# Turning the first queries by full-height TensorE transposes, with fewer small products ahead of them

## The chip, the cores and the metric

The program runs on one core of one Trainium2 chip. The metric is the device time of one execution in microseconds (us), taken from several executions of the same program. A profiled execution gives the trace, in which every instruction of the core has a start and a duration. TensorE (PE) multiplies matrices and writes into PSUM, VectorE (DVE) and ScalarE (ACT) copy, add and evaluate functions, GpSimd (POOL) adds, and the DMA queues move data between main memory and SBUF. The trace also has one record for every DMA packet, those that bring a core its own instructions included.

## The reference

A linear attention block comes first, then two dense layers with a leaky ReLU between them. Batch and heads are 8 and 8, the sequence has 576 positions and the head 64 columns; the dense layers go from 512 to 2048 and back for 4608 tokens. Both weight matrices arrive as 64-bit floats, because a 32-bit array is multiplied by a 64-bit scalar.

```python
def _attn_ref(q, k, v, g_norm):
    kv = np.einsum('bhsd,bhse->bhde', k, v)
    out = np.einsum('bhsd,bhde->bhse', q, kv)
    rms = np.sqrt(np.mean(out * out, axis=-1, keepdims=True) + 1e-06)
    return (out / rms * g_norm).astype(np.float32)

def _moe_ref(x, w_in, w_out):
    h = x @ w_in
    g = np.maximum(0.01 * h, h)
    return (g @ w_out).astype(np.float32)

def reference(**kwargs):
    ...
    attn_out = _attn_ref(**attn_kwargs)
    # bridge: (B,H,S,D) -> (B*S, H*D)
    B, H, S, D = attn_out.shape
    x = np.ascontiguousarray(attn_out.transpose(0, 2, 1, 3)).reshape(B * S, H * D)
    return _moe_ref(x=x, **moe_kwargs)
```

## The kernel before

The first batch of attention stands alone at the start, because no dense layer can run before its result is there. TensorE contracts over partitions, so the product of q with kv needs q with its 64 head columns on the partitions. Later batches get that from a DVE transpose; the first one gets it from TensorE. The heads go in pairs `p` (four of them), two heads `l` in a pair, and a pair's tile `q_in` holds the two heads on partitions 0 to 63 and 64 to 127, with 9 (`J`) rows of 64 columns on each partition.

```python
def load_first():                      # cut: the tiles' homes
    for way, to, src, ts, p in (
            ("a", q_ins, q, qs, 0), ("s", q_ins, q, qs, 1), ("a", q_ins, q, qs, 2),
            ("s", q_ins, q, qs, 3), ("a", k_ins, k, ks, 0), ("s", v_ins, v, vs, 0),
            ("g", k_ins, k, ks, 1), ("g", v_ins, v, vs, 1), ("a", k_ins, k, ks, 3),
            ("s", v_ins, v, vs, 3), ("g", k_ins, k, ks, 2), ("g", v_ins, v, vs, 2)):
        ...
        to[0, p] = load_two({"a": nc.scalar, "s": nc.sync, "g": nc.gpsimd}[way],
                            src[0, 2 * p:2 * p + 2], ts[p])

zeros = view(g_all[0], 0, NT)          # NT = 512
nc.vector.memset(zeros[:, :64], 0.0)
nc.vector.memset(zeros[:, 64:], 0.0)
...
def half_of(p, i):                     # which half of the partitions a head's result takes
    return i ^ (p & 1)

def attention_kv(b, m, kv_ps):         # kv of the pairs 2m and 2m+1: 36 products of 64x64
    two = [(k_ins.pop((b, p)), v_ins.pop((b, p)), p) for p in (2 * m, 2 * m + 1)]
    for j in range(J):
        for i in range(2):
            for k_in, v_in, p in two:
                r, c = 64 * i, 64 * half_of(p, i)
                matmul(kv_ps[p % 2][c:c + 64, m, :], lhsT=k_in[r:r + 64, j, :],
                       rhs=v_in[r:r + 64, j, :], start=(j == 0), stop=(j == J - 1))
```

The first attention begins with products of zeros, which raise TensorE's clock, then turns q, forms kv, and goes on to the normalised result x. Every result of a product passes through PSUM and is copied from there.

```python
def first_attention():
    idle = ps_m.tile([P, NT], F32, tag="hd", name="idle_ps")

    def keep_warm(to=idle):
        matmul(to, lhsT=zeros[:, :P], rhs=zeros, start=True, stop=True)

    for _ in range(15):
        for i in range(4):
            r = slice(E * i, E * i + E)
            matmul(idle[r, :64], lhsT=zeros[r, :E], rhs=zeros[r, :64], start=True, stop=True)
    keep_warm()
    ...
    for p in range(NP):
        q_in = q_ins.pop((0, p))
        q_ps = ps_m.tile([P, J - 1, 64], F32, tag=("ha", "hb", "hc", "ha")[p], name="q_ps")
        for j in range(J):
            for l in range(2):
                r, c = slice(64 * l, 64 * l + 64), 64 * half_of(p, l)
                matmul((q_ps[:, j, :] if j < J - 1 else rest[p % 2][:, p // 2, :])[c:c + 64],
                       lhsT=q_in[r, j, :], rhs=ident[r, r], start=True, stop=True)
        to = qT[:, p, :].rearrange("p (t j) -> p j t", j=J)
        h = J // 2
        nc.scalar.copy(to[:, :h, :], q_ps[:, :h, :])
        nc.vector.tensor_copy(to[:, h:J - 1, :], q_ps[:, h:, :])
    for i in range(2):
        nc.vector.tensor_copy(
            qT.rearrange("p a (t j) -> p a t j", j=J)[:, i::2, :, J - 1], rest[i])
    for m in range(2):
        if m:
            keep_warm()
        attention_kv(0, m, kv_ps)
    for j in range(3, 7):
        load_w(j)
    w0 = rounding(0)                   # 64-bit weights to 32-bit, a few ACT and DVE steps
    next(w0, None)                     # two ACT steps
    copy_kv(0, kv_ps)
    next(w0, None)
    ...                                # o_products: 32 products, q with kv, into four banks
    for l in range(2):
        square(0, l)                   # ACT
        keep(0, l)                     # DVE, two copies
        add_up(0, l)                   # TensorE, sums over the columns of a head
    next(w0, None)                     # DVE
    square(1, 0); add_up(1, 0)
    root(0); turn(0)                   # ACT, TensorE
    next(w0, None)                     # DVE
    invert(0)                          # DVE
    ...
    spread(0); add_up(1, 1); root(1); turn(1); keep(1, 0); keep(1, 1)
    scale(0, 0); invert(1); scale(0, 1); spread(1)
    for l in range(2):
        scale(1, l)
    for j in range(1, 5):
        round_w(j)
```

After this the first block of the dense layers runs with plain products (`h_ps`, `o_acc`), and later blocks with a scheme of seven products in place of eight.

Of the kernel before, what the change touches and what calls it, by code (L numbers as in the profile page):

```python
# [9 lines left out]
F32 = mybir.dt.float32  # L10
# [13 lines left out]
def kernel(  # L24
# [36 lines left out]
    nc = tc.nc  # L61
    B, H, S, D = q.shape
    DM, DF = w_in.shape
    P = 128
    NE = DM // P
    E = 32
    NP = H // 2
    J = S // 64
    T = S // 32
    NT = 4 * P  # L70
    NB = B * S // NT
    N2 = NT // 2
# [1 line left out]
    NC = DF // 2 // (U * P)  # L74
    SLOPE = 0.01
    EPS = 1e-6
    assert H * D == DM and S == 64 * J and D == 64 and 2 * E == D and H == 8 and NP * E == P and B * S == NB * NT
    assert DM // 2 == N2 and NE == 4

    consts = ctx.enter_context(tc.tile_pool(name="consts", bufs=1))  # L80
# [7 lines left out]
    ps_m = ctx.enter_context(tc.tile_pool(name="ps_m", bufs=1, space=bass.MemoryType.PSUM))  # L88

    pin = tc.keep_in_program_order  # L90
# [14 lines left out]
    def view(t, lo, *shape):  # L105
        n = 1
        for d in shape:
            n *= d
        t = t[:, lo:lo + n]
        names = "abcd"[:len(shape)]  # L110
        return t.rearrange(f"p ({' '.join(names)}) -> p {' '.join(names)}",
                           **dict(zip(names, shape))) if len(shape) > 1 else t
# [4 lines left out]
    def matmul(*args, **kw):  # L117
        pin(nc.tensor.matmul(*args, **kw))  # L118
# [4 lines left out]
    def half_of(p, i):  # L123


        return i ^ (p & 1)
# [58 lines left out]
    zeros = view(g_all[0], 0, NT)  # L185
    nc.vector.memset(zeros[:, :64], 0.0)
    nc.vector.memset(zeros[:, 64:], 0.0)
    ident = consts.tile([P, P], F32, name="ident")
# [33 lines left out]
    def load_f64(src, eng):  # L222
        a, n = src.shape[-2:]
        n //= 2
        raw = next(raw_homes).bitcast(U32).rearrange("p (n two) -> p n two", two=2)
        load(raw.rearrange("p (a n) two -> p a (n two)", a=a), src, eng)
        return raw
# [41 lines left out]
    def load_w(j, *eng):  # L269
        eng = eng or (nc.sync,)  # L270
        dst, src = w_jobs[j]
        if w_in.dtype == I64:
            w_raws[j] = load_f64(src.bitcast(U32), eng)
        else:
            load(dst, src, eng)

    def rounding(j):
        if w_in.dtype == I64:
            yield from round_f64(w_jobs[j][0], w_raws.pop(j))
# [43 lines left out]
    def kv_tiles():  # L323
        return [ps_att.tile([P, NP // 2, D], F32, tag="att", name="kv_ps") for _ in range(2)]
# [116 lines left out]
    def first_attention():  # L441


        idle = ps_m.tile([P, NT], F32, tag="hd", name="idle_ps")

        def keep_warm(to=idle):
            matmul(to, lhsT=zeros[:, :P], rhs=zeros, start=True, stop=True)

        for _ in range(15):
            for i in range(4):
                r = slice(E * i, E * i + E)
                matmul(idle[r, :64], lhsT=zeros[r, :E], rhs=zeros[r, :64], start=True, stop=True)
        keep_warm()
        qT = qTs[0] = work.tile([P, NP, S], F32, tag="qT", name="qT")
        kv_ps = kv_tiles()
        rest = [ps_m.tile([P, NP // 2, 64], F32, tag=t, name="rest_ps") for t in ("oc", "oa")]
        for j in range(1, 3):
            load_w(j)  # L460
        for p in range(NP):
            q_in = q_ins.pop((0, p))
            q_ps = ps_m.tile([P, J - 1, 64], F32, tag=("ha", "hb", "hc", "ha")[p], name="q_ps")
            for j in range(J):
                for l in range(2):
                    r, c = slice(64 * l, 64 * l + 64), 64 * half_of(p, l)
                    matmul((q_ps[:, j, :] if j < J - 1 else rest[p % 2][:, p // 2, :])[c:c + 64],
                           lhsT=q_in[r, j, :], rhs=ident[r, r], start=True, stop=True)
            to = qT[:, p, :].rearrange("p (t j) -> p j t", j=J)
            h = J // 2  # L470
            nc.scalar.copy(to[:, :h, :], q_ps[:, :h, :])
            nc.vector.tensor_copy(to[:, h:J - 1, :], q_ps[:, h:, :])
        for i in range(2):
            nc.vector.tensor_copy(
                qT.rearrange("p a (t j) -> p a t j", j=J)[:, i::2, :, J - 1], rest[i])
        for m in range(2):
            if m:
                keep_warm()
# [3 lines that stand above are left out]
        w0 = rounding(0)  # L482
# [5 lines that stand above are left out]
        x = block(0)  # L488

        o_ps = [[ps_m.tile([P, 2, N2], F32, tag=t, name="o_ps") for t in tags]  # L490
                for tags in (("hb", "hd"), ("oa", "oc"))]
        squares = [[spare(NT, "sq").rearrange("p (e n) -> p e n", e=2) for _ in range(2)]
                   for _ in range(2)]
        roots = [work.tile([P, 2, 2, NP], F32, tag="rms", name="roots", bufs=2) for _ in range(2)]
        flat = [work.tile([64, N2], F32, tag="t2k", name="flat", bufs=3) for _ in range(2)]
        sum_ps = [ps_att.tile([P, NT], F32, tag="att", name="sum_ps") for _ in range(2)]
        inv_ps = [ps_m.tile([P, 2, N2], F32, tag=t, name="inv_ps") for t in ("ha", "hc")]
        for half in range(2):
            for e in range(2):
                o_products(0, half * N2, half * N2 + N2, e,  # L500
                           [o_ps[half][l][:, e, :] for l in range(2)])

        def square(half, l):
            pin(nc.scalar.activation(squares[half][l], o_ps[half][l], func=AF.Square))

        def keep(half, l):
            for e in range(2):
                to, o = x[:, 2 * l + e, half * N2:half * N2 + N2], o_ps[half][l][:, e, :]
                if half == 0:
                    pin(nc.vector.tensor_scalar(to, o, g_sb[:, e:e + 1], None, op0=ALU.mult))  # L510
                else:
                    pin(nc.scalar.activation(to, o, func=AF.Copy, scale=g_sb[:, e:e + 1]))

        def add_up(half, l):

            for e in range(2):
                matmul(sum_ps[half][E * l:E * l + E, :N2], lhsT=group,
                       rhs=squares[half][l][:, e, :], start=(e == 0), stop=(e == 1))

        def root(half):  # L520

            pin(nc.scalar.activation(flat[half], sum_ps[half][:64, :N2], func=AF.Sqrt,
                                     scale=1.0 / D, bias=eps_sb[:64]))

        def turn(half):
            for t in range(2):
                matmul(turned(half)[:, t, :, :], lhsT=flat[half][:, t * P:t * P + P],
                       rhs=ident[:64, :64].rearrange("p (l i) -> p l i", l=2)[:, :, :NP],
                       start=True, stop=True)

        def turned(half):
            return sum_ps[half][:, N2:N2 + 4 * NP].rearrange("p (t l a) -> p t l a", t=2, l=2)

        def invert(half):
            pin(nc.vector.reciprocal(roots[half], turned(half)))

        def spread(half):

            for l in range(2):
                for t in range(2):  # L540
                    for p in range(NP):
                        matmul(inv_ps[half][E * p:E * p + E, l, t * P:t * P + P],
                               lhsT=roots[half][:, t, l, p:p + 1].to_broadcast([P, E]),
                               rhs=ident, start=True, stop=True)

        def scale(half, l):
            to = x[:, 2 * l:2 * l + 2, half * N2:half * N2 + N2]
            pin(nc.vector.tensor_tensor(
                to, to, inv_ps[half][:, l, :].unsqueeze(1).to_broadcast([P, 2, N2]), op=ALU.mult))

        for l in range(2):
            square(0, l)
            keep(0, l)
            add_up(0, l)
        next(w0, None)
        square(1, 0)
        add_up(1, 0)
        root(0)
        turn(0)
        next(w0, None)  # L560
        invert(0)
        for _ in w0:
            pass
        square(1, 1)
        spread(0)
        add_up(1, 1)
        root(1)
        turn(1)
        keep(1, 0)
        keep(1, 1)  # L570
        scale(0, 0)
        invert(1)
        scale(0, 1)
        spread(1)
# [4 lines that stand above are left out]
# [360 lines left out]
    x_sides, _, sums, _ = sides_x(1)  # L939
# [123 lines left out]
```

## Time and profile before

The time before is 942.53 us, the median of three executions (942.1 to 942.6). The profiled execution took 942.25 us, of which the program's instructions span 940.5 us.

| Engine | Busy us | Share of the span | Instructions |
|---|---|---|---|
| PE, matmul | 920.1 | 98% | 7076 |
| PE, weight load | 779.1 | 83% | 7076 |
| DVE | 616.0 | 65% | 992 |
| ACT | 327.5 | 35% | 659 |
| POOL | 317.7 | 34% | 318 |

One product of 32-bit numbers in the code stands as two matmul records and two weight loads in the trace, so 7076 records are half as many products. A group of matmul records can overlap in the trace, because small products in different parts of the array run side by side. A line of the timeline begins with the start and the length in us, and ends, in brackets, with the idle time before it and what the profile takes to have ended it. "issue" there is idle time in which the engine waited for nothing that the profile shows.

### The profile page before, as it was taken

To read this page: it belongs to the slowest core of one execution; us is meant where nothing else is said; L and a number is where in the kernel's file an instruction comes from. 1 tells how busy PE (TensorE), PEld (TensorE's weight loads), DVE (VectorE), ACT (ScalarE), POOL (GpSimd) and SP (SyncE) were. 2 spreads that over 40 slices of the span, in tenths; PEclk is the share of its full clock that TensorE was granted. 3 is DMA by queue.
4 is the path that set the end of the run, shared out by engine and by line. 5 is a ranking of instruction groups with operands and counts; after the bars stand their busy time and mean duration, and the time that the engine had idled before them with its cause. 6 is when DMAs were issued, how large, how long until landed. Compare 5 with 4: busy or idle time off the path is not lost.

```text
span 940.5 us, 17989 instructions
## 1 busy us (share of the span) xinstructions
PE 920.1 (98%) x7076; PEld 779.1 (83%) x7076; DVE 616.0 (65%) x992; ACT 327.5 (35%) x659; POOL 317.7 (34%) x318
## 2 busy tenths in 40 slices
PE   7999999999999999999999999999999999999997
PEld 5544447788998899889998999989988999899996
DVE  3866994576457876587657865687558745654554
ACT  3544633242134332533343323342344232223320
POOL 2000364977522532236221611172225322532222
PEclk9999999999999999999999999999999999999999
DMA  8989916885598679856895589658755675567632
GB/s 271 246 211 220 267 61 188 275 296 163 181 312 260 182 211 304 257 164 200 286 287 173 171 280 297 193 169 262 236 154 176 196 219 188 174 199 220 187 108 67
DMA packets 90067, 200.05 MB, mean 213 GB/s; under 512 B 9856, under 2 KB 42112, under 8 KB 89984
## 3 DMA queue, kind: packets, MB, share of 16 engines
q1 hardware_dynamic: 79392, 186.85, 66.3%
q10 hardware_dynamic: 10144, 10.88, 3.4%
q8 instruction: 56, 0.92, 0.4%
q0 software_dynamic: 448, 1.18, 0.3%
q14 instruction: 27, 0.22, 0.1%
HBM read 172.39 MB, written 26.48 MB: 211 GB/s over the span
## 4 chain that ended last, share of the span: by engine, by line
PE 86%; DVE 8%; DMA 3%; issue 1%; POOL 1%; ACT 1%; SPq 0%; DVEq 0%; ACTq 0%; POOLq 0%
PE o_a L118 21%; PE o_c L118 17%; PE h_ha L118 10%; PE h_hc L118 8%; PE h_hb L118 7%; PE h_hd L118 6%; PE o_acc L118 4%; PE h_ps L118 4%; PE kv_ps L118 2%; PE h_c L118 2%; PE h_d L118 2%; PE o_ps L118 1%; PE h_a L118 1%; DMA pairs<-in_v_dram 1%; DVE o L582 1%
## 5 line engine op out<-in xcount | busy, mean ns | idle before, releaser
L582 POOL TENSOR_TENSOR gs<-g 128x512 f32<-128x512 f32 x64 | 81.3, 1289 | 446.7 <-ACT g L753 446.7
L582 DVE TENSOR_TENSOR o<-o_c,o 128x512 f32<-128x512 f32 x85 | 58.5, 688 | 108.2 <-PE o_c L118 108.1
L753 ACT ACTIVATE g<-g 128x512 f32<-128x512 f32 x124 | 78.2, 631 | 122.9 <-DVE g L582 122.9
L118 PE MATMUL o_a<-pairs,gs 128*128 128x256 f32 x496 | 117.3, 379 | 0.0
L582 DVE TENSOR_TENSOR o<-o_a,o 128x512 f32<-128x512 f32 x100 | 68.7, 687 | 71.2 <-PE o_a L118 71.1
L817 ACT COPY w_all<-h_ha 128x512 f32<-128x512 f32 x84 | 48.7, 580 | 189.8 <-PE h_ha L118 181.0
L118 PEld LDWEIGHTS o_a<-pairs,gs 128*128 128x128 f32 x496 | 90.0, 190 | 9.9
L118 PE MATMUL o_a<-w,g 128*128 128x256 f32 x248 | 59.9, 384 | 4.7 <-DVE o L582 4.1
L118 PEld LDWEIGHTS h_ha<-stage,w_all 128*128 128x128 f32 x448 | 58.8, 192 | 2.9
L118 PE MATMUL o_c<-w,g 128*128 128x256 f32 x248 | 59.7, 383 | 0.0
L118 PE MATMUL o_c<-pairs,gs 128*128 128x256 f32 x248 | 59.2, 381 | 0.0
L118 PE MATMUL o_a<-pairs,g 128*128 128x256 f32 x248 | 59.2, 381 | 0.0
L118 PE MATMUL h_ha<-stage,w_all 128*128 128x128 f32 x448 | 59.0, 275 | 0.0
L118 PE MATMUL o_acc<-w,g 128*128 128x512 f32 x128 | 58.3, 598 | 0.7 <-ACT g L898 0.7
L118 PE MATMUL o_c<-w,gs 128*128 128x256 f32 x248 | 58.7, 379 | 0.0
L118 PE MATMUL h_ps<-xT,w_all 128*128 128x512 f32 (+1 forms) x136 | 57.9, 570 | 0.2 <-DVE w_all L255 0.2
L582 DVE TENSOR_TENSOR g<-g,pairs 128x512 f32<-128x512 f32 x84 | 55.6, 689 | 1.9
L118 PEld LDWEIGHTS o_a<-w,g 128*128 128x128 f32 x248 | 44.9, 190 | 13.9 <-DVE o L582 7.8
L582 POOL TENSOR_TENSOR pairs<-w_all 128x512 f32<-128x512 f32 x8 | 11.1, 1383 | 125.7 <-ACT cut L244 106.9
L118 PEld LDWEIGHTS o_c<-w,g 128*128 128x128 f32 x248 | 44.9, 190 | 8.4 <-issue 3.1
L118 PEld LDWEIGHTS o_a<-pairs,g 128*128 128x128 f32 x248 | 45.0, 190 | 6.5 <-DVE w_all L582 0.9
L118 PEld LDWEIGHTS o_c<-pairs,gs 128*128 128x128 f32 x248 | 44.9, 190 | 6.5 <-issue 1.4
(202 smaller groups left out, 1980.6 us busy)
## 6 DMA issues: line engine op xcount, KB each, us to landing
w_all<-w SPq DMA_DIRECT2D x196, 448.0 KB, 4.1
pairs<-w SPq DMA_DIRECT2D x56, 512.0 KB, 4.4
out_dram<-o ACTq DMA_DIRECT2D x36, 256.0 KB, 4.6
v_in<-in_v_dram SPq DMA_DIRECT2D x29, 288.0 KB, 5.3
k_in<-in_k_dram SPq DMA_DIRECT2D x28, 288.0 KB, 5.8
q_in<-in_q_dram SPq DMA_DIRECT2D x56, 144.0 KB, 6.1
q_in<-in_q_dram SPq DMA_DIRECT2D x56, 140.0 KB, 6.0
w<-stage SPq DMA_DIRECT2D x12, 512.0 KB, 4.5
```

Of the source, the lines that this page charges most:

```text
L118: pin(nc.tensor.matmul(*args, **kw))
L582: ins = eng.tensor_tensor(out_, a, b_, op=ALU.subtract if minus else ALU.add)
L753: nc.scalar.activation(t, t if src is None else src, func=AF.Prelu, alpha=SLOPE)
L817: nc.scalar.copy(q[:, at], banks[tag])
```

## The change

The first queries are turned by transposes that take both heads of a pair at once: 128 partitions by 64 columns become 64 partitions by 128 columns, in one instruction of TensorE's transpose kind. All of it lands on PSUM partitions 0 to 63, and the copies to SBUF move each head to the half of the partitions that it belongs to. The 60 small zero products in front are left out; a second wide zero product takes their place, and zero products of half the width stand between the pairs. The purpose is to shorten TensorE's stream of instructions before kv.

```diff
-        def keep_warm(to=idle):
-            matmul(to, lhsT=zeros[:, :P], rhs=zeros, start=True, stop=True)
-        for _ in range(15):
-            for i in range(4):
-                r = slice(E * i, E * i + E)
-                matmul(idle[r, :64], lhsT=zeros[r, :E], rhs=zeros[r, :64], start=True, stop=True)
+        def keep_warm(n=NT):
+            matmul(idle[:, :n], lhsT=zeros[:, :P], rhs=zeros[:, :n], start=True, stop=True)
+        keep_warm()
         keep_warm()
         ...
-        rest = [ps_m.tile([P, NP // 2, 64], F32, tag=t, name="rest_ps") for t in ("oc", "oa")]
+        rest = ps_m.tile([64, NP, P], F32, tag="oc", name="rest_ps")
         ...
+        def move(p, l, to, of):
+            c = 64 * half_of(p, l)
+            eng = (nc.scalar.copy, nc.vector.tensor_copy)[l]
+            eng(qT[c:c + 64, p, :].rearrange("p (t j) -> p j t", j=J)[:, to, :],
+                of[:, :, 64 * l:64 * l + 64])
         for p in range(NP):
             q_in = q_ins.pop((0, p))
-            q_ps = ps_m.tile([P, J - 1, 64], F32, tag=("ha", "hb", "hc", "ha")[p], name="q_ps")
+            banks = [ps_m.tile([64, 4, P], F32, tag=t, name="q_ps")
+                     for t in (("ha", "hb"), ("hc", "oa"))[p % 2]]
             for j in range(J):
+                to = banks[j // 4][:, j % 4, :] if j < 8 else rest[:, p, :]
+                pin(nc.tensor.transpose(to, q_in[:, j, :], ident))
+            if p + 1 < NP:
+                keep_warm(N2)
+            for i in range(2):
                 for l in range(2):
-                    r, c = slice(64 * l, 64 * l + 64), 64 * half_of(p, l)
-                    matmul((q_ps[:, j, :] if j < J - 1 else rest[p % 2][:, p // 2, :])[c:c + 64],
-                           lhsT=q_in[r, j, :], rhs=ident[r, r], start=True, stop=True)
-            to = qT[:, p, :].rearrange("p (t j) -> p j t", j=J)
-            h = J // 2
-            nc.scalar.copy(to[:, :h, :], q_ps[:, :h, :])
-            nc.vector.tensor_copy(to[:, h:J - 1, :], q_ps[:, h:, :])
-        for i in range(2):
-            nc.vector.tensor_copy(
-                qT.rearrange("p a (t j) -> p a t j", j=J)[:, i::2, :, J - 1], rest[i])
+                    move(p, l, slice(4 * i, 4 * i + 4), banks[i])
+        for p in range(NP):
+            for l in range(2):
+                move(p, l, slice(8, 9), rest[:, p:p + 1, :])
```

The kv products, their waits, the order of everything after them and all loads are as before.

## The prediction

> **What bounds the kernel now.** I read the table of stretches first (length in us; then for each engine busy us and instructions; clock, DMA share, GB/s).
>
> ```profile
> 0.00:32.00 32.00, 24.40 (x580) 18.81 (x580) 13.38 (x32) 14.12 (x27) 5.16 (x14) 1.00 0.89 262
> 32.00:150.00 118.00, 117.21 (x504) 52.78 (x505) 94.76 (x167) 51.40 (x107) 21.42 (x16) 1.00 0.78 199
> 150.00:900.00 750.00, 744.34 (x5812) 677.47 (x5811) 490.75 (x768) 256.24 (x517) 282.52 (x282) 1.00 0.71 220
> ```
>
> From 32 us on TensorE is busy 99% of the time, and the change touches nothing there. The first 32 us hold 7.6 us of TensorE's idle time, and only they can change. So the whole effect is the shift of the first dense product (h_ps, 28.16 us). Next I read TensorE's timeline of that stretch, and one window of the DMA packets.
>
> ```profile
> 1.06 4.35 PE L118 MATMUL idle_ps<-g 32*32 32x64 f32 x122 [1.06 <-DVE g L186]
> ...
> 9.27 0.27 PE L118 MATMUL q_ps<-ident,early 64*64 64x64 f32 x2 [1.09 <-issue]
> ...
> 11.34 1.38 PE L118 MATMUL kv_ps<-v_in,k_in 64*64 64x64 f32 x72 [0.68 <-DMA k_in<-in_k_dram]
> 12.65 1.12 PE L118 MATMUL idle_ps<-g 128*128 128x512 f32 x2
> 14.28 0.52 PE L118 MATMUL kv_ps<-pairs 64*64 64x64 f32 x8 [0.50 <-DMA pairs<-in_v_dram]
> 15.79 1.16 PE L118 MATMUL kv_ps<-pairs 64*64 64x64 f32 x64 [0.99 <-issue]
> 17.43 2.05 PE L118 MATMUL o_ps<-qT,kv 64*32 64x256 f32 x64 [0.48 <-DVE kv L321]
> 20.76 1.91 PE L118 MATMUL sum_ps<-sq,group 128*32 128x256 f32 x12 [1.28 <-ACT sq L504]
> ...
> 28.16 3.72 PE L118 MATMUL h_ps<-xT,w_all 128*128 128x256 f32 x16
> ```
>
> Two stops are "issue": in the middle of a pair of q at 9.27, and eight records into the second kv at 15.79, where no data is missing. A third is hidden: sum_ps at 20.76 is put down to ACT, yet the first square began at 18.70 and ended near 19.3. The packets of the instruction queue explain all three.
>
> ```profile
> q8 instruction: 1, 0.02, 6.0%
> ```
>
> That is the window from 13 to 14 us. The queue has one packet of 16,384 bytes at 6.98, 13.46, 18.37 and 23.50 us, each about 1.0 us long, and TensorE goes on some 1.3 to 1.4 us after the first three ended (7.98 to 9.27, 14.42 to 15.79, 19.39 to 20.76). Counted in the timeline, 223 matmul records stand before the first stop, 348 before the second, 476 before the third: 125 and 128 apart, which with a weight load each is 256 instructions of 64 bytes, one packet. So TensorE starves for instructions three times. From going on to the next packet took 4.19, then 2.58, then 2.74 us: the packet of a block is asked for when the block before it is entered.
>
> **What the Trainium skill says.** "Runtime: NRT & Kernel Launch", section "Instruction fetch mechanics", has blocks of 16 KiB, 256 instructions, fetched by the engine's own DMA queue one ahead; the trace agrees. It calls the crossing "mostly hidden"; here three crossings show, with small products used up faster than blocks come. "TensorE: Matmul & The Clock Gate", section "Terms", has a transpose mode four times faster for 32-bit data; no run here shows it yet, but each transpose compiles to one matmul and one weight load where a product needs two of each. Its Part 4 says that transposes don't count as activity for the clock. Its Part 1 gives half clock until about 3.4 us of activity; the trace grants the full clock at 4.09 us, after zero products from 1.06.
>
> **The change part by part.** Counts: zero products fall from 122 records to 4 + 3 x 2 = 10, q from 144 to 36 (36 transposes at one record each). Together 266 become 46, so TensorE's stream is 440 instructions, nearly two blocks, shorter before kv. The compiled program agrees: 6856 records in place of 7076.
>
> Block ends stay put in the stream: before, they lie at records 95 (128 less than 223), 223, 348 and 476. Counting waits in as well, record 93 of the changed kernel is the first end, 47 records into the first kv; the next is record 219, 27 of 64 into o_ps; the third is record 347, in the first h_ps; the fourth lies among long products of 0.43 us.
>
> Front: the wide zero product waits for the whole memset (ends 1.48), so starts near 1.5. Eight records of this width take 3.43 us in the first block, 0.43 each at full clock, so 0.86 at half clock; three of those and a short fourth reach to about 4.7. q's first pair lands at 4.69. So the transposes begin about 4.8 where q began at 5.34; nothing hangs on that.
>
> Turning: 16 copies of 64 partitions by 256 plus 8 small ones, half on each engine. A 128x256 copy takes 0.62 us on either engine; I take the same for 64 partitions, and 0.3 for a small one. ACT is issuing weight loads until about 6.2; eight copies at a pitch of 0.53 (three ACT squares take 1.57) end near 10.5. In the kernel before, a DVE copy starts when the ACT copy of the same bank ends (7.16 to 7.19), so I let DVE trail by one, to 11.2. The eight small ones share one tile and alternate: 11.2 + 7 x 0.3 = 13.3. The last transposes need the second pair's banks, free near 9.2, so TensorE is through by about 10. kv starts at 11.34 because k lands at 11.30. qT is needed by o_ps after 16. All of this stays hidden.
>
> Step 1, kv. The first end is crossed about 11.6, when nothing has to be fetched in a hurry. The second kv starts at 14.28 and runs through like the first: last operand lands at 14.42, 1.3 us more, done 15.75 instead of 17.01. Minus 1.26.
>
> Step 2, o_ps. Copies of kv take 0.42 as before: o_ps starts at 16.17. Its record 27 needs the block asked for at 11.6: 2.6 to 4.2 to the packet, 1.0 for it, 1.4 to go on, so 16.6 to 18.2, near 16.9 in the middle. Needed near 16.7. The first square needs 32 records, so about 17.4 without a stop. ACT has two rounding steps behind a weight that lands at 16.31; they ran from 16.41 to 17.63 and stay there. The first square moves from 18.70 to 17.63: minus 1.07.
>
> Step 3, sums. No block end stands before sum_ps any more. The DVE row sets the pace: square ends 18.26, four keeps (1.66), two rounding steps (1.1), so inversion at 21.0, where it was 23.32. TensorE's half (sum 19.45, root 0.47, turn and hop 0.96) is ready at 20.9. The sum of steps 1 to 3 is minus 2.3, and everything behind it (spread, second half, scaling) keeps its lengths: h_ps at 25.85.
>
> Afterwards: could the weights hold h_ps back? Weight jobs 1 to 6 landed at 17.91, 20.77, 23.00, 24.95, 27.73 and 29.68 and were taken up by ACT at 27.40, 28.53, 29.68, 30.82, 36.25 and 37.40; slack of over 5 us, and loads gated by kv move forward too. ACT waits for no weight's DMA between 28 and 150. The 0.73 us wait of o_acc at 143.15 hangs on a DVE chain which TensorE's own o_ps at 108 started, so it shifts along. 942.5 - 2.3 = 940.2.
>
> **The rivals.**
> - The fetch comes late. At the slowest seen (4.19 + 0.96 + 1.37 = 6.5 after 11.6) o_ps stops until 18.1, the first square is at about 18.5, and only step 3 remains: minus 1.2 to 1.4, about 941.2. For it: DMA is busy until 14.4. Against it: the later packets came after 2.6 to 2.7.
> - The clock falls. The zero products start later, and transposes may not count, so 4.9 to 11.3 us has only three pieces of 0.43 us of plain products. At half clock kv's second half (1.3), o_ps (2.0) and sums take up to twice as long: plus 1 to plus 4, about 942 to 945. Against it: by the steps above one of the added zero products falls into about every 3.4 us, and the clock here stayed full over 17.5 to 24 us with only about half the time busy.
> - Copies bind. With a 64-partition copy over 1 us, the turning would reach past 16 us and hold o_ps. The time would be about 942. Against it: 3 us of slack.
> - Nothing shows: kv is set by landing (14.42), so someone reading only the chain of waits would expect zero. The chain speaks against this, since the stop is after the landing.
>
> **Range and chances.** The main case, 65%, gives 940.0 to 940.4; the late fetch, 20%, about 941.2; the clock or copies, 15%, 942 and up. Executions differ by 0.25. I centre on 940.4 with 939.5 to 942.0. Two per cent are 18.9 us, more than all that the first 20 us hold, so chances of either side are one in a hundred or less.
>
> **What would show it.** Right: instruction packets near 14.5 and 20 only, no "issue" stop before kv's end, kv done near 15.8, sum_ps following the first square, h_ps near 25.9, and a span 2.3 shorter with equal lengths after it. Wrong: a stop of over 1 us in o_ps (step 2), a granted clock of 0.5 after 5 us, two matmul records for a transpose, ACT or DVE still copying q at 16 us, or an h_ps that starts earlier with the gain given back before 150 us.

## The result

| Comparison | Changed kernel, median us (range) | Before, median us | Ratio, 95% interval |
|---|---|---|---|
| first, the one predicted | 938.76 (937.86 to 939.59) | 942.57 | 0.9958, 0.9940 to 0.9975 |
| second | 941.29 (938.05 to 944.15) | 942.70 | 0.9985, 0.9974 to 0.9996 |
| third | 940.65 (937.83 to 942.73) | 942.16 | 0.9978, 0.9968 to 0.9988 |

The change makes the kernel faster by 0.15% to 0.42%, that is by 1.4 to 3.8 us between the medians. The prediction was 940.4 with a range of 939.5 to 942.0; the measured 938.76 lies 0.7 us below the range. The two later comparisons, made as experiments, lie inside it. Both kernels spread over 4 us and more from one execution to the next, which three executions of before had not shown, and that spread turns out to be half of the story.

TensorE's timeline of the changed kernel, first 32 us (start, length, what, and in brackets the idle time before it and what ended it):

```profile
1.53 3.78 PE L118 MATMUL idle_ps<-g 128*128 128x512 f32 x4 [1.53 <-DVE group L291]
5.21 1.69 PE L472 MATMUL q_ps<-ident,q_in 128*64 128x128 f32 x8
...
10.11 1.04 PE L472 MATMUL q_ps<-ident,early 128*64 128x128 f32 x8
10.98 0.27 PE L472 MATMUL rest_ps<-ident,early 128*64 128x128 f32 x1
11.19 1.28 PE L118 MATMUL kv_ps<-v_in,k_in 64*64 64x64 f32 x72
12.39 1.12 PE L118 MATMUL idle_ps<-g 128*128 128x512 f32 x2
13.45 1.28 PE L118 MATMUL kv_ps<-pairs 64*64 64x64 f32 x72
15.24 1.17 PE L118 MATMUL o_ps<-qT,kv 64*32 64x256 f32 x27 [0.51 <-DVE kv L321]
17.90 1.49 PE L118 MATMUL o_ps<-qT,kv 64*32 64x256 f32 x37 [1.49 <-issue]
19.32 1.93 PE L118 MATMUL sum_ps<-sq,group 128*32 128x256 f32 x12
...
26.87 3.72 PE L118 MATMUL h_ps<-xT,w_all 128*128 128x256 f32 x16
```

The stops at 9.27 and 15.79 are gone, and so is the hidden one before sum_ps. One stop is left, 27 records into o_ps, where the count in the instruction stream put it. The window from 15 to 16 us holds the first packet of the instruction queue:

```profile
q8 instruction: 1, 0.02, 7.4%
```

It starts at 15.18 and takes 1.18 us; TensorE goes on 1.54 us after its end. So the first h_ps is at 26.87 where it was 28.16, 1.29 us earlier. Yet the two profiled spans differ by 4.24 us (940.50 and 936.26). I lined up DVE's instructions from the end of both traces and followed the distance between each and its twin:

```
time in the trace of before   changed kernel ahead by   DVE instruction there
 23.32                        1.29                      inversion of the roots
174.19                        1.51                      qT
176.69                        2.32                      copy of kv
572.72                        2.61                      weight sums
929.50                        4.24                      o, in the last block
```

Four steps beside the first one, all far behind the changed lines. The largest is in the last block. Before, then changed (the bracket is the wait for GpSimd's sums):

```profile
921.76 1.89 PE L118 MATMUL h_c<-w,g 128*128 128x256 f32 x8
925.90 3.56 PE L118 MATMUL h_d<-pairs,gs 128*128 128x256 f32 x8 [2.25 <-POOL gs L582]
```

```profile
919.09 1.89 PE L118 MATMUL h_c<-w,g 128*128 128x256 f32 x8
923.23 1.99 PE L118 MATMUL h_d<-pairs,gs 128*128 128x256 f32 x8 [2.25 <-POOL gs L587]
```

The wait is the same, but the eight records behind it took 3.56 us in place of 1.99: the granted clock was 0.5 from 925.69 to 929.11 in the trace of before, and 1.0 there in this one. The other sizeable step is the kv product of the next batch but one. Before, then changed:

```profile
174.09 0.33 PE L118 MATMUL kv_ps<-v_in,k_in 64*64 64x64 f32 x2
175.38 1.27 PE L118 MATMUL kv_ps<-v_in,k_in 64*64 64x64 f32 x70 [0.96 <-DMA v_in<-in_v_dram]
```

```profile
172.80 1.52 PE L118 MATMUL kv_ps<-v_in,k_in 64*64 64x64 f32 x72
```

Here v landed in time in one trace and 1 us late in the other. A smaller difference lies in the products `o_a`, which wait until DVE has added the last ones to its running sum `o`. Before, then changed (us in total, number of waits, the longest):

```profile
PE o_a L118 <- DVE o L582: 4.1, 6, 1.3
```

```profile
PE o_a L118 <- DVE o L587: 3.8, 6, 1.3
```

It sits in one of the six, which ends at 418.71 before and at 416.04 in the changed kernel: 0.96 and 0.61 us.

The mean granted clock of the four first executions of the changed kernel points at the same thing as the last block: 938.20 us at 0.999, 937.86 at 1.000, but 939.59 and 939.32 at 0.998.

### The profile page after: what moved, and what is told of

Same layout as the page of the kernel before. It is cut to its first block, busy times and chain, and to the rows that moved or that the text cites. A ratio compares the mean times of both kernels' runs of the same rounds, so it can differ in the third digit from the quotient of the medians.

```text
span 936.3 us, 17564 instructions
## 1 busy us (share of the span) xinstructions
PE 919.6 (98%) x6856; PEld 776.6 (83%) x6856; DVE 618.2 (66%) x998; ACT 330.3 (35%) x667; POOL 317.9 (34%) x318
## 3 DMA queue, kind: packets, MB, share of 16 engines
q0 software_dynamic: 448, 1.18, 0.3%
## 4 chain that ended last, share of the span: by engine, by line
PE 88%; DVE 7%; DMA 3%; issue 1%; ACT 1%; POOL 0%; DVEq 0%; ACTq 0%
PE o_a L118 22%; PE o_c L118 17%; PE h_ha L118 10%; PE h_hc L118 8%; PE h_hb L118 8%; PE h_hd L118 6%; PE o_acc L118 4%; PE h_ps L118 4%; PE kv_ps L118 2%; PE h_d L118 2%; PE h_a L118 2%; PE h_c L118 2%; PE h_b L118 1%; PE o_ps L118 1%; DMA stage<-in_moe_w_in_dram 1%; DVE w_all L587 1%
```

## The experiments

The theory that they test: TensorE starves for instructions at block ends of 256; the change helps by moving these ends; what lies behind 32 us belongs to the execution and not to the change.

**Both kernels once more, and each half of the change alone.** The kernel before and the changed kernel ran without an edit. "Zero products alone" is before with this edit, so with the old products for q:

```diff
-        for _ in range(15):
-            for i in range(4):
-                ...                    # 60 small zero products
         keep_warm()
+        keep_warm()
```

"Transposes alone" is the changed kernel with the 60 small zero products and one wide one in front, as before, and without the zero products between the pairs.

> The kernel before once more, no edit: how much of the 4.2 us between the two profiled spans comes back without any change. Theory A (start only): the changed kernel is ahead by 1.3 us at its first h_ps because of the fetched instructions, and the rest (1.0 us at a kv product near 175 us that waited for v, 1.6 us of half clock near 926 us) is luck of one execution. Then this run shows the kv wait near 175 absent or of another length, and its executions split into spans about 1.6 us apart that go with the mean clock (0.998 against 1.000). Theory B (all belongs to the change): this run repeats the wait of about 1.0 us near 175 and the half clock near 926 in every execution, clock 0.998 each, 942 to 943.

> The changed kernel once more, no edit. Theory A: 937.9 to 939.6, with executions of clock 0.998 about 1.4 us slower than those of 0.999 or 1.000, as in its first four; the stop in o_ps 27 records in comes back at the same record, since it belongs to the instruction stream, with a length that may differ by 1 us. Theory B: no half clock near 924 in any profile, and 938.0 plus or minus 0.3. If the stop sits at another record, it is no fetch of instructions.

> Only the small zero products left out (a second wide one in their place), q turned by the old products. Fetch theory: block ends are crossed at matmul records near 94, 222 and 350, which here lie in pair 3 of q, at the start of the second kv, and 56 of 64 into o_ps. No stop in the second kv; one stop before the last records of o_ps, lasting until about 17 to 20 us; first h_ps between 26 and 27.5 us, so most of the gain of the whole change with none of its transposes: 938.5 to 940.5. Rival (the transposes are what gives the gain, by taking TensorE time away): the time stays at that of before, 942, and h_ps at about 28. Landing rival: kv ends earlier only if k and v land earlier than 14.4.

> Only the transposes: the 60 small zero products and one wide one in front stay as before, no zero products between pairs. Fetch theory: block ends near records 95, 223 and 351 lie in the zeros, 65 of 72 into the first kv, and 47 of 64 into o_ps. No stop in either kv (the second block was asked for at about 3.5 us), a stop inside o_ps at record 47 until about 17 to 19 us, but the first squares (record 32) are not held: first square near 17.5, h_ps 25.8 to 27, time 938 to 940. If zero products between the transposes are needed for the clock, its granted clock falls to 0.5 for one window of 3.4 us between 5 and 20 us, and h_ps is later by 1 us or more. Rival (fetch plays no part): h_ps as in the changed kernel, 26.9, with the stop again at record 27.

Before came to 942.51 against 942.70 (ratio 0.9995, 0.9982 to 1.0007). Its trace is that of the slowest of the twelve executions (944.70). From TensorE's timeline:

```profile
14.02 0.46 PE L118 MATMUL kv_ps<-pairs 64*64 64x64 f32 x8 [0.75 <-DMA pairs<-in_v_dram]
17.72 1.98 PE L118 MATMUL kv_ps<-pairs 64*64 64x64 f32 x64 [3.24 <-issue]
20.18 3.69 PE L118 MATMUL o_ps<-qT,kv 64*32 64x256 f32 x64 [0.48 <-DVE kv L321]
```

The stop is at the same record, 8 into the second kv, but lasts 3.24 us where it was 0.99, after an instruction packet that came at 15.04. And after it the clock is at half (16.85 to 23.68), so o_ps takes 3.69 us in place of 2.05. h_ps came at 31.20, three us later than in the first trace of the same program. The kv wait near 175 was 0.36 in place of 0.96, and the half clock of the last block was there again. So theory A is right that the wait near 175 varies (0.15 to 0.96 in the three traces of before, none to 0.46 in the four of the changed kernel), and neither theory had thought of the spread of the start itself.

The changed kernel's second trace has the stop at record 27 again (1.68 us), h_ps at 26.65, a wait of 0.23 near 173, and the half clock at 923.30, with which it is 1.74 us behind its first trace. So far that is theory A. But the median of 941.29 is above what either theory gave (937.9 to 939.6, and 938.0).

The mean clock of each execution shows where the rest went. In the fourteen traces a mean of 0.999 or 1.000 goes with no stretch of half clock before the last product, 0.998 with one, 0.996 with two and 0.994 with three. Of the 20 executions of the changed kernel twelve have 0.998 or more and none 0.994; of the 41 of before fourteen have 0.998 or more, and nine 0.994. At 0.998 the medians are 940.4 and 941.1. So the change gains 0.7 us at equal clock, and its executions also have fewer stretches at half clock, which theory A had called luck. Whether they were spared at the start or at the end can't be told without their traces.

Zero products alone: 940.11 (0.9980, 0.9964 to 0.9996).

```profile
11.02 0.70 PE L118 MATMUL idle_ps<-g 128*128 128x512 f32 x1
13.90 1.01 PE L118 MATMUL idle_ps<-g 128*128 128x512 f32 x1 [2.19 <-issue]
14.84 2.20 PE L118 MATMUL kv_ps<-pairs 64*64 64x64 f32 x72
```

The stop sits one record before the second kv, where record 222 was expected, and is 2.19 us long; I had expected none there, because I took the block to be back by then, and one 56 records into o_ps, which did not come. It is followed by half clock (13.54 to 16.95), and still h_ps comes at 27.13. The second kv ends at 17.04, no earlier than in the first trace of before (16.95); the gain stands at the sums, which start at 19.61 and not at 20.76, with no stop in front of them. Leaving out the small zero products alone, without any transpose, gives a gain of the size of the whole change on the same chip (0.9980 beside 0.9985).

Transposes alone: 938.45 (0.9963, 0.9934 to 0.9992, from five executions, so a wide interval).

```profile
14.26 1.40 PE L118 MATMUL kv_ps<-pairs 64*64 64x64 f32 x72 [1.09 <-DMA pairs<-in_v_dram]
16.12 2.47 PE L118 MATMUL o_ps<-qT,kv 64*32 64x256 f32 x64 [0.47 <-DVE kv L321]
...
25.92 3.72 PE L118 MATMUL h_ps<-xT,w_all 128*128 128x256 f32 x16
```

No stop in kv, a short one of 0.2 us 43 records into o_ps (47 expected), h_ps at 25.92. The clock stayed full from 4.15 us to the last block without any zero product between the pairs.

One thing behind 32 us does go with the change. The wait of `o_a` near 418 us is 0.96 to 0.98 in the four traces that turn q by the old products, zero products alone included, and 0.60 or 0.61 in the ten that turn it by transposes. Why these 0.35 us go was not tried.

**The stop made to move.** If block ends are what counts, added work must help when it moves an end to a harmless place, and hurt when it moves it to a bad one. The edit, with 10 and with 5 rounds of four; the changed kernel ran again beside the first:

```diff
+        for _ in range(10):            # or 5
+            for i in range(4):
+                r = slice(E * i, E * i + E)
+                matmul(idle[r, :64], lhsT=zeros[r, :E], rhs=zeros[r, :64], start=True, stop=True)
-        keep_warm()
         keep_warm()
```

> The changed kernel, no edit, as the measure for the three runs beside it. Theory A: the gain at the first h_ps is 1.3 to 1.6 us against a before of 28.2 (more against a before whose own stop in kv was longer), the half clock near 923 us is there in some executions and not in others, and the time against before comes to a ratio near 0.998. Theory B: the ratio of the first comparison, 0.9958, comes back.

> The changed kernel with work ADDED in front: 40 small zero products in place of one of the two wide ones, 78 more matmul records. Fetch theory: block ends move to the start of pair 2 of q (crossed near 7 us), to record 23 of the second kv (its block lands near 12 to 13, so no stop), and behind the first sums. The stop in o_ps (1.5 to 1.7 us in two profiles of the changed kernel) is gone, the first square comes near 17.5 in place of 18.6, held by the weight that lands at 16.3, and h_ps near 25.7 in place of 26.7 to 26.9: faster by about 1 us although it does more. Rival 1 (the stop is a wait for a copy of q or of kv, or anything tied to o_ps itself): the stop stays at record 27 and nothing is gained. Rival 2 (fewer instructions are better, simply): slower by what is added, up to 2 us.

> The changed kernel with 20 small zero products in place of one wide one, half of the run with 40. Fetch theory: the first block end is now just inside the first kv (record 93 of the stream, 9 records into kv), the second at record 63 of 72 of the second kv. Its block is asked for near 10.5 to 11.3 us and takes about 6.5 us or more to be used, so the stop moves into the second kv, nine records before its end, until 17 to 18.6 us; h_ps between 27.5 and 29, later than in the changed kernel and up to 3 us later than with 40. The time is 940.5 to 942.5. Rival (the small products help by holding the clock): between the changed kernel and the run with 40, 938.9 to 940.6, with no stop in kv. On the second question: the last k and v landed at 12.5 to 12.9 us in the five profiles whose first instruction packet came after 11 us, and at 13.9 to 16.2 in the eight where one came before 9.1. If the packet delays them, they land near 12.8 here, as its packet is late; if the small zero products do, near 14.

With 40 small products more: 938.86 (0.9964, 0.9954 to 0.9974) beside 940.65 for the changed kernel on the same chip.

```profile
14.02 1.40 PE L118 MATMUL kv_ps<-pairs 64*64 64x64 f32 x72 [0.46 <-DMA pairs<-in_v_dram]
15.88 2.06 PE L118 MATMUL o_ps<-qT,kv 64*32 64x256 f32 x64 [0.47 <-DVE kv L321]
17.99 2.03 PE L118 MATMUL sum_ps<-sq,group 128*32 128x256 f32 x12
...
25.65 3.72 PE L118 MATMUL h_ps<-xT,w_all 128*128 128x256 f32 x16
```

All of kv, o_ps and the sums run through, although the second kv starts later than in the changed kernel (12.81 to 13.85), and h_ps is at 25.65 where 25.7 was expected. With 20 more: 942.40 (0.9990, 0.9975 to 1.0006), which is the time of before.

```profile
14.35 1.16 PE L118 MATMUL kv_ps<-pairs 64*64 64x64 f32 x62
17.86 0.44 PE L118 MATMUL kv_ps<-pairs 64*64 64x64 f32 x10 [2.35 <-issue]
18.74 3.67 PE L118 MATMUL o_ps<-qT,kv 64*32 64x256 f32 x64 [0.43 <-DVE kv L321]
```

The stop has moved to record 62 of the second kv (63 expected), ends at 17.86 (17 to 18.6 expected), and h_ps is at 29.76, 0.8 later than expected because half clock follows (19.01 to 22.42). Nought, 20 and 40 products more give 26.65 to 28.82 (four traces), 29.76 and 25.65: no cost per instruction explains that order, and the place of the block ends does. The clock does not either: it was full from 8.77 us with 20 and from 4.21 with 40, but the second kv started at 14.35 and 14.02, so a later full clock in front makes 0.3 of the 4.1 us between them.

The changed kernel's third trace shows how a longer wait for the block turns into more. Its stop at record 27 was 2.71 us, and the table of two stretches reads (length; PE, PEld, DVE, ACT and POOL busy us and instructions; clock, DMA share, GB/s):

```profile
14.79:18.20 3.41, 1.06 (x27) 0.58 (x25) 0.00 (x0) 1.21 (x2) 0.00 (x0) 1.00 1.04 239
18.20:21.62 3.42, 3.06 (x39) 1.36 (x40) 1.74 (x5) 1.32 (x3) 0.00 (x0) 0.50 1.06 233
```

A stretch of 3.41 us with TensorE busy for 1.06 is followed by one at half clock, and h_ps came at 28.82. In this comparison, too, the change leaves more executions at 0.999 or 1.000 (9 of 22, before 2 of 47), and at 0.998 the medians are 940.8 and 941.6.

**The end held warm.** In the changed kernel, and in the kernel before, four products that nobody reads fill the gap in the last block. In a fourth kernel they go with the transposes alone, in a fifth with the 40 small products.

```diff
             elif i == 4:
                 sums(1)
+            if i == 2 and n + 1 == NC * (NB - 1):
+                spare_ps = ps_m.tile([P, 2, N2], F32, tag="oc", name="spare_ps")
+                for _ in range(4):
+                    matmul(spare_ps[:, 0, :], lhsT=g_sides[1][:, 0, :],
+                           rhs=w_sides[1][:, 0, :], start=True, stop=True)
```

> The changed kernel with four products nobody reads, 1.73 us of TensorE in all, in the gap of 2.25 us near 921 us where TensorE waits for GpSimd's sums. Theory A (the clock falls to half for 3.4 us when a clock window holds that gap, and costs 1.6 us in those executions): the granted clock stays 1.0 until after the last product, and the time falls by 0.6 to 1.6 us against the changed kernel on the same chip, its slower executions going. Rival (the half clock near 923 comes from something else, or costs nothing because the end is set by GpSimd and the last stores): clock still 0.5 there, or no change in time within 0.3.

> The kernel before with the four filling products at its end, and nothing else. Theory A (the half clock near 926 us has nothing to do with the change; it comes when a clock window holds most of the gap): clock 1.0 there, time 0.8 to 1.6 us under before on the same chip, ratio 0.998 to 0.999. Theory B (the changed kernel avoids it in some other way): no gain here, or a half clock at another place of the end.

> Transposes with the 60 zero products kept, and the four filling products at the end: the two things that the runs so far point to as best. Theory A: h_ps at 25.9 to 26.2 as in the run with transposes alone, clock 1.0 throughout, time 1 to 2 us under the changed kernel on the same chip, 936.5 to 938. Rival (the run with transposes alone was luck in its few executions): no better than the changed kernel with the filling products.

> The changed kernel with 40 small zero products in front and the four filling products at the end. If the two gains are of different places and add: h_ps near 25.7, clock 1.0 until after the last product, 937.0 to 938.0 at the median, ratio 0.995 to 0.9955 against before. If the slow executions came from the start alone, no better than with the 40 products alone (ratio 0.9964).

The changed kernel so filled:

```profile
921.45 1.89 PE L118 MATMUL spare_ps<-w,g 128*128 128x256 f32 x8
923.88 1.99 PE L118 MATMUL h_d<-pairs,gs 128*128 128x256 f32 x8 [0.54 <-POOL gs L587]
```

The wait shrinks to 0.54 and the eight records behind it take 1.99. In all traces with the filling products (these four and the next) the clock stays full until the last product; of the nine traces without them, only the first one of the changed kernel has a full clock there. The changed kernel went from 940.65 to 938.99 (0.9967, 0.9956 to 0.9978, beside 0.9978), close to the 1.6 us that the traces show, though the intervals overlap. Before gained less than expected: 941.55 against 942.23, ratio 0.9995, 0.9984 to 1.0005, which settles nothing by itself; its trace gains 1.63 us at the last block, and half clock at the start (17.79 to 21.21) stands against it.

Transposes alone with the filling: 938.01 (0.9956, 0.9939 to 0.9973), from six executions. Its trace drew a bad start: k and v landed at 16.23, half clock followed, and h_ps came at 29.00, so its 940.32 was the slowest of the six. The 40 small products with the filling: 937.30 (0.9959, 0.9946 to 0.9973), 937.06 to 939.11, clock 1.000, h_ps at 25.68. This is the best version with its reason known; its interval overlaps that of the 40 products alone, so the last 1.5 us are shown by the trace and not by the ratio.

**What bounds the start next.** With the stop gone, the first square stands behind ACT's two rounding steps, which wait for a weight that lands near 16. They were moved behind the first root:

```diff
         w0 = rounding(0)
-        next(w0, None)
         copy_kv(0, kv_ps)
-        next(w0, None)
         ...
         square(1, 0); add_up(1, 0); root(0)
+        next(w0, None)
         turn(0)
         ...                            # its DVE steps follow invert(0) and scale(0, 0)
```

> As the run beside it, and ACT's two rounding steps for the first weight are moved behind the first root, so that the first square no longer stands behind a weight that lands near 16.2 us. What bounds the path after the fetch stop is gone should be that weight: the first square then comes near 16.6 in place of 17.5, the first inversion near 19.9 in place of 20.9, h_ps near 24.6 in place of 25.7, and the median is about 1 us under the run beside it. Rival (a third block end, asked for near 14 us, stands before turn(0), or DVE's order binds): h_ps moves by less than 0.4.

No gain: 937.63 (0.9959, 0.9946 to 0.9973; two of the 16 executions took over 943), h_ps at 25.78 beside 25.68. The first square began at 17.47, though it no longer waited for a weight, since in this trace the second kv started at 14.34, after k and v that landed at 14.20. It stood 1.27 us behind the start of o_ps, as in the first trace of before, and 1.49 in the run beside it, so the weight had held it by 0.2 us and not by 1. So the landing of k and v and the weight lie close together as the bound, and taking away one leaves the other.

## Why the prediction was off

| Program | first instruction packet | last k, v landed | stop, at | h_ps |
|---|---|---|---|---|
| before, three traces | 6.67 to 6.98 | 13.88 to 14.82 | 0.99, 1.32, 3.24, kv | 28.16, 29.07, 31.20 |
| changed, four traces | 15.04 to 15.83 | 12.68 to 12.89 | 1.19, 1.49, 1.68, 2.71, o_ps | 26.97, 26.87, 26.65, 28.82 |
| zero products alone | 11.37 | 12.53 | 2.19, before kv | 27.13 |
| 20 more | 15.20 | 12.56 | 2.35, kv | 29.76 |
| transposes alone, two traces | 6.78, 7.01 | 14.12, 16.23 | 0.2, o_ps; none seen | 25.92, 29.00 |
| 40 more, three traces | 8.68 to 9.05 | 13.88 to 14.20 | none | 25.65 to 25.78 |

(The filling products at the end don't touch these columns; "before" and "changed" include the traces with them.)

Two steps failed. In the start it was step 2: the stop was not removed but moved from kv into o_ps. What put the time outside the range was the term for the spread of executions. That the first four executions came so low is in part luck: all of them had a mean clock of 0.998 or more, and eight of the next 20 had 0.996. Nor do the two later medians inside the range (941.29 and 940.65) confirm the sum: the gain there is 1.4 and 1.5 us where I had 2.1, and it holds terms that the sum did not have, the 0.35 us near 418 and the half clock.

- Where the change works: right for the start, not for what lies behind it. I had everything behind 32 us keep its length; the wait near 418 fell from 0.96 to 0.61 us. In the start nothing moves before h_ps that isn't carried on, the block ends were at the records counted (27 of 64 into o_ps), and the other kernels that stopped did so within four records of a place counted for them.
- Step 1, kv without a stop: right in kind, done at 14.73 for 15.75, because k and v landed 1.5 us earlier than in before. I had taken the landing as fixed.
- Step 2, o_ps: the step that failed in the start. I put 2.6 to 4.2 us, near 3, between asking for a block and its packet, and 5.3 until TensorE goes on, so no stop to speak of. The traces don't show the moment of asking. From the start of record 93, the first behind the block end (10.96 to 12.30 in the four traces of the changed kernel), it was 3.0 to 4.9 us to the packet (15.04 to 15.83) and 5.7 to 7.6 until TensorE went on, and in the first trace the records in front of the stop ended at 16.41, where I had put the need at 16.7. So the stops are 1.2 to 2.7 us; one of over 1 us was my own sign of being wrong. The late fetch, which got 20%, was the main case: the first square moved by 0.13 us (18.70 to 18.57) and not by 1.07.
- Step 3, the sums: right, and in the first pair of traces nearly the whole gain. From the first square to h_ps the path is 8.30 us where it was 9.46, a gain of 1.16. The start as a whole gave 1.29 in the first pair of traces, where the rival had said 1.2 to 1.4.
- "Executions differ by 0.25": the term that put the measured time outside the range. It was read from three executions. In truth the end has a half clock in some executions and not in others (1.6 us), and the start of before lost 0.9 or 3.0 us more in its two later traces. The wait for v near 175 (0.96 us) stood in the trace of before as well, and I took it to keep its length.
- The copies, hidden: right. The last ends at 14.58, before kv is copied at 14.81; a copy of 64 partitions by 256 takes 0.60 to 0.66 us. The margin was 0.2 us and not 3, since the copies ended 1.3 us later than I had put them and kv came earlier.
- The transposes: one record each, as said, but the reason is instructions alone. Nine of them take about 1.1 us (10.11 until kv starts at 11.19).
- The clock in front: full at 6.56 us (4.55 to 7.46 in the four traces), which goes against a sign I had given, no half clock after 5 us. The first eight transposes took 1.69 us in place of 1.04, and TensorE was through with them at 11.25 and not near 10. It cost little: in the second trace, with full clock at 5.11, h_ps came 0.22 us earlier.

## What to carry to other kernels

When many small products follow each other, count records between the "issue" stops and look for the packets of the instruction queue: if both keep step with 256 instructions, the place of the block ends is a thing to tune, and a few dummy products in an idle front can do more than fewer instructions in the middle. Before a change of a few us is judged, look at the granted clock of several executions and compare those at equal clock too, and treat a wait of 2 us for another engine in front of the last products as a place where TensorE's clock is lost. Make the range from several executions' traces, and not from the spread of three times.

## What was not expected of the hardware

- A late block costs twice. Stretches of 3.41 us in which TensorE was busy for 0.46 to 1.58 us were followed by half clock in six places at the start and eight at the end; stretches with 1.73, 1.94 and more at the start were not. The busy share gives no single sharp limit: the end of the changed kernel's first trace kept the full clock with 1.52 us of wide products. The stretches begin at another time in each execution, so the same gap costs 1.6 us in one and nothing in the next. The Trainium skill, "TensorE: Matmul & The Clock Gate", Part 1, warns of idle gaps over about 3.4 us; here one of 2.25 us was enough in eight of nine traces.
- Where an instruction packet came before 9.1 us, the last k and v landed at 13.88 to 16.23 (eight traces); where the first came after 11 us, at 12.53 to 12.89 (six traces). The kernel with 20 small products more has them in front and its packet late, and landed at 12.56, so it isn't the small products. That the packet of 16 KiB, 1.0 us on the queue, holds up transfers that are spread over the engines would fit, but how it does so wasn't tried.
- The zero products between the pairs, meant to keep the clock, weren't needed at that place in the two traces without them: it stayed full through about 5 us with nothing but transposes. In the one with the filling, the stretch from 7.57 to 10.98 us held no product at all; TensorE was busy with transposes for 2.30 us of it, and the clock stayed full until 17.81. Part 4 of the same page says that transposes don't count as activity in the same way; in this trace they kept the clock. Both kernels had the 60 small zero products in front (over at 5.44), and the one with the filling lost the clock later, at 17.81, after TensorE had waited for k and v until 16.23.
- The Trainium skill, "Runtime: NRT & Kernel Launch", section "Instruction fetch mechanics", calls the crossing of a block end mostly hidden. With products as small as these, nine of the fourteen traces have a stop of 0.99 to 3.24 us at one.
